# Attention and two gated layers on one core: how v of a pair of heads is brought into SBUF

## Chip, cores and metric

The kernel runs on one core of one Trainium2 chip. The metric is the device time of one execution in microseconds (us), as the median of several runs. A profile is one more execution, recorded instruction by instruction. Its span runs from the first instruction to the last, and its device time is a little longer than the span.

## What is computed

Three layers follow each other, on a batch of 4 sequences of 576 positions:

```python
# attention: 8 heads of 64, window of 128 positions, slope per head
scores = scale * np.matmul(q, k.transpose(0, 1, 3, 2))
scores = np.where((rel >= 0) & (rel < 128), scores + bias[None], -1e9)
attn = softmax(scores)                    # along the keys
x = np.matmul(attn, v)                    # heads side by side: 4 x 576 x 512
# first gated layer, 512 -> 1024 -> 512
h = np.maximum(x @ w_in, 0.0)
x = h * sigmoid(conv3(h)) @ w_out         # conv3: 3 taps along the sequence
# second gated layer, 512 -> 512 -> 512
out = sigmoid(conv5(x)) * (x @ w_val) @ w_out2   # conv5: 5 taps, causal
```

All inputs and the output are float32.

## The kernel before

**Units.** The work is cut into eight units (b, u): each of the 4 sequences in two parts, the second a little shorter or longer than the first. A unit goes through attention, `hidden` (w_in, ReLU, 3 taps, gate), `mixed` (w_out, 5 taps), `valued` (w_val and gate) and `output` (w_out2). While PE runs the dense layers of one unit, the attention of the next unit is interleaved with it.

**Dense layers.** `dense` and `prod` (L825 to L844) make each float32 product out of three matmuls of a high part and a low part: L830, L831 and L832 (`pm<-x,win`, `pm<-g,wout` and so on). ACT, DVE and POOL then work on the result: ACT scales (L415, L416, L432), DVE adds taps (L422) and, for a few taps, POOL adds them (L433, from a product that ACT made). At the end POOL makes the low part of the next operand (L437, `g<-t,g`), which PE needs for its L831 matmuls.

**Attention.** The first sequence uses `attention` (one pair of heads at a time, v loaded by L593). The other three use `duo`: two pairs of heads, r and its neighbour, at once. A unit has two duos, so there are 12 of them. One duo:

- q and k of two pairs are loaded (L697), into a ring of four buffers `qk`, two in the tile `qkt` and two in the tile `pp`.
- v of the two pairs is loaded into the tile `vr`, by two transfers (L715). Each chunk is 64 positions of the sequence. The 64 partitions 0 to 63 hold the first pair of heads, 64 to 127 the second. The two transfers take the even and the odd chunks. A duo of the first part has 5 chunks (3 and 2, that is 192 KB and 128 KB), one of the second part 6 (192 KB twice).
- POOL scales `vr` in place (L718, `vr<-vr,vup`), casts it to 16 bits (L408 through `cast`, `v<-vr`) and takes the remainder (L721, `v<-vr,v`). Both halves lie in `v16`. There is one `vr` and one `v16`: the next duo's transfers wait until L721 has read `vr`, and the next cast until the PV product has read `v16`.
- PE makes scores (L754), DVE and ACT the softmax (L564, L569, POOL L573 and DVE L575), ACT and DVE the two 16 bit halves of the probabilities (L781, L783), and two DMA transposes for each section (L788, `pp<-pp`) turn them. PE then makes the PV product (L811), which ACT and DVE move into x (L556, L558).

In DRAM v has the layout `vN[b, position in a block of 128, pair of heads, block, two heads x 64]`, so that each row is contiguous over the blocks of a pair.

**What sets the order.** Nothing is scheduled by the hardware across engines: every engine takes its instructions in the order of the program, and waits where a semaphore says so. A planner (`Program`) makes this order. Every operation is added with the engines that may run it, an assumed duration, and what it reads and writes. `forward` simulates a list schedule with assumed latencies, `backward` sets priorities from it, and `order` does so 1 + TRIES times, from the ninth time on with random changes of the priorities. The 12 shortest are replayed with random delays, and the best of these is the program. All transfers are issued by SP: `sync` (L401) takes an assumed transfer time, which it multiplies by 1.33, and an assumed issue time of SP, 475 ns unless given. In the assumption a transfer occupies one common DMA resource for its transfer time, whatever its shape.

POOL, too, is one queue: where L718 waits for v, the L433, L437, L408 and L573 behind it wait as well.

Of the kernel before, what the change touches and what calls it, by code (L numbers as in the profile page):

```python
# [26 lines left out]
TURN = 1  # L27
FILL = 80000.0
RW = 2 * WC
TRIES = 100  # L30
NATIVE = ()
LATE = (11,)

# [11 lines left out]
class Program:  # L45
# [165 lines left out]
    def order(self):  # L211
# [4 lines left out]
        rng, found = random.Random(1), []  # L216
        for i in range(1 + TRIES):
            if i:
# [64 lines left out]
def pool_t(n, two=False, ap=0):  # L283
    return 2.06 * n + 185 if two else 0.83 * n + 83 * ap + 160
# [15 lines left out]
def attention_moe_moe_kernel(  # L300
# [14 lines left out]
    nc = tc.nc  # L315
# [10 lines left out]
    def st(name, shape, dt):  # L326
        return sb.tile(shape, dt, name=name)
# [41 lines left out]
    vr = st("vr", [128, 6, 128], F32)  # L369
# [31 lines left out]
    def sync(fn, prio, reads=(), writes=(), xfer=0.0, issue=475.0):  # L401
        return pg.add("SP", issue, fn, prio, reads, writes, 0.0, xfer * 1.33)
# [275 lines left out]
    def users(keys):  # L678
        return {o for k in keys for o in [pg.writer.get(k)] + pg.readers.get(k, []) if o is not None}

    def duo(b, u, r, prio, step):
# [7 lines left out]
        early = prio - 3.149 * step * 2  # L689
        q_t, k_t, qk = [], [], []  # L690
        for y in range(2):
            t, key = ring_qd.next()
            old = users(QALIAS[ring_qd.at]) if ring_qd.i <= len(ring_qd.t) else set()
            first_, then = qk0[b, 2 * r + y], qk1[b, 2 * r + y]
            parts = [(0, 768, first_, 0), (768, 832, then, 768), (832, 960, then, 0)] if u == 0 else [(0, 960, then, 128)]
            for x, (a, e, src, f) in enumerate(parts):
                sync(lambda t=t, a=a, e=e, src=src, f=f: nc.sync.dma_start(out=t[:, a:e], in_=src[:, f:f + e - a]),  # L697
                     early, (), ((key, x),) if u == 0 else tuple((key, z) for z in range(3)), (e - a) * 1.43, 600.0).preds.update(old)
            qk += [(key, z) for z in range(3)]
            q_t.append([t[:, 128 * i:128 * i + 128] for i in range(4)] + ([t[:, 832:960]] if u == 0 else []))  # L700
            k_t.append(t[:, 512:832] if u == 0 else t[:, 576:960])
# [6 lines left out]

        n = 128 * nch
        vin, va, vb = vr[:, 0:nch], v16[:, 0, 0:nch], v16[:, 1, 0:nch]  # L710
        vk = (("vf0", 0), ("vf0", 1))
        old_v = users(("vf0",)) if nth == 0 else set()
        for x in range(2):
            c, at_, m = k0 + x, x * odd, (odd, nch - odd)[x]
            sync(lambda c=c, at_=at_, m=m: nc.sync.dma_start(  # L715
                out=vr[:, at_:at_ + m], in_=vN[b, 64 * (c % 2):64 * (c % 2) + 64, 2 * r:2 * r + 2, c // 2:c // 2 + m, :].rearrange(
                    "k y t c -> y k (t c)")), early + 6000.0, (), (("vf0", x),), 182.0 * m, 600.0).preds.update(old_v)
        pg.add("POOL", pool_t(n, False, 1), lambda: nc.gpsimd.tensor_scalar(vin, vin, s_up, 0.0, op0=ALU.mult, op1=ALU.add),  # L718
               prio, ((VS[b], 1, 0), (VS[b], 1, 1)), vk)
        cast(vin, va, n, prio, vk, (("v16", 0),) + (("vf1",) if nth == 0 else ()), ("POOL",))  # L720
# [7 lines left out]
        old = users(PALIAS) if nth == 0 else set()  # L728
# [3 lines left out]
        for gi, g in enumerate(secs):  # L732
# [4 lines left out]
            for y in range(2):  # L737
                o, sk = held[y]
                c = 0
# [24 lines left out]
            a, e = items[0][2], items[-1][2] + 1  # L764
            turned_over(stt[:, 2, a:e], stt[:, 1, a:e], norm, pr, tuple((stk, 1, x[2]) for x in items), ((stk, 2, gi),))
            for y, i, n, s, nkey, _, sk, on in items:
# [4 lines left out]
                if nth in LATE and y:  # L771
                    t, tk = ring_t.next()
                    t = t[:, 0:nkey]
                    tc3 = t.rearrange("p (t c) -> p t c", c=64)
                    pg.add("ACT", act_t(nkey, True, 1), lambda s=s, t=t, ri=ri: nc.scalar.activation(
                        out=t, in_=s, func=AF.Copy, scale=ri), pr, (on, (stk, 2, gi)), (tk,), bank=sk)
                    cast(tc3, hi, nkey, pr, (tk,), (("P", 0, i, y),))
                    pg.add("POOL", pool_t(nkey, True), lambda tc3=tc3, hi=hi, lo=lo: nc.gpsimd.tensor_tensor(
                        out=lo, in0=tc3, in1=hi, op=ALU.subtract), pr, (tk, ("P", 0, i, y)), (("P", 1, i, y),))
                    continue  # L780
                pg.add("ACT", act_t(nkey, True, 1), lambda sc=sc, hi=hi, ri=ri: nc.scalar.activation(  # L781
                    out=hi, in_=sc, func=AF.Copy, scale=ri), pr, (on, (stk, 2, gi)), (("P", 0, i, y),), bank=sk).preds.update(old)
                pg.add("DVE", dve_t(nkey, 1), lambda sc=sc, hi=hi, lo=lo, ri=ri: nc.vector.scalar_tensor_tensor(  # L783
                    out=lo, in0=sc, scalar=ri, in1=hi, op0=ALU.mult, op1=ALU.subtract),
                    pr, (on, (stk, 2, gi), ("P", 0, i, y)), (("P", 1, i, y),), bank=sk).preds.update(old)
            ca, ce = max(0, 3 * g[0] - base), 3 * g[-1] + 3 - base
            for q in range(2):
                sync(lambda q=q, ca=ca, ce=ce: nc.sync.dma_start_transpose(  # L788
                    out=ptd[:, q, ca:ce, :], in_=pd[:, q, ca:ce, :].rearrange("p a c -> p (a c)")),
# [182 lines left out]
    def attentions(b, u, base, T):  # L972
        if b < TURN:
            for p in range(NP):
                attention(b, u, p, base + T * (p / NP * 0.72 + 0.081), T * 0.72 / NP / (len(BLK[b, u]) + 1))
            return
        for r in range(NP // 2):
            duo(b, u, r, base + T * (r / 2 * 0.72 + 0.081), T * 0.72 / 2 / (3 + u))
# [14 lines left out]
    t, todo = T0, UNITS  # L993
    for i, (b, u) in enumerate(todo):
        base = t
        for f in steps:
            t = f(b, u, t, rate)
# [86 lines left out]
```

## Time and profile before

| what | value |
|---|---|
| median of 3 runs | 467.54 us (lowest 467.28) |
| profiled execution | 470.1 us |
| its span | 468.3 us |
| mean granted clock of TensorE in it | 0.949 |
| PE busy | 415.5 us (89%) |
| DVE, ACT busy | 298.4 us, 298.5 us (64% each) |
| POOL busy | 231.3 us (49%) |

The engines are PE (TensorE matmuls), PEld (its weight loads), DVE (VectorE), ACT (ScalarE), POOL (GpSimd) and SP (SyncE, which issues all transfers here). A granted clock of 1.00 is TensorE's higher level, 2.4 GHz, and 0.50 the lower, 1.2 GHz; a number between is a mean over a stretch that has both. The DMA share is the mean busy share of the core's 16 DMA engines; over short stretches with transposes it can come out above 1. An arrow in square brackets names how long an engine sat idle before an instruction and what ended that.

### The profile page before, as it was taken

The numbers are of one execution on the slowest core, as the hardware profiler recorded it, in microseconds if no ns is written. First come the engines' busy times: TensorE is split into PE (matmuls) and PEld (weight loads), VectorE is DVE, ScalarE is ACT, GpSimd is POOL, SyncE is SP. The second block draws the span as 40 slices with busy tenths as digits, with TensorE's granted clock in tenths as the row PEclk, the third lists the DMA queues.
The fourth block names the chain that finished last, engine by engine and source line by source line (L and its number), as shares of the span: only waits on it lengthen the run. The fifth ranks groups of instructions, "written<-read, shape, count | busy, mean of one in ns | idle before, by whom it ended". The sixth has DMA issues, their size and how long they took to land.

```text
span 468.3 us, 10804 instructions
## 1 busy us (share of the span) xinstructions
PE 415.5 (89%) x3925; PEld 390.4 (83%) x3925; DVE 298.4 (64%) x930; ACT 298.5 (64%) x906; POOL 231.3 (49%) x360
## 2 busy tenths in 40 slices
PE   7899998999599769699795779999969799999997
PEld 6778888899489769699694679999958799999896
DVE  3689988598565577565744527795754648662651
ACT  5799997487456556466735337876755448753743
POOL 3589997156463065143372316533643617651632
PEclk9999999999979979799977979999999899999999
DMA  7878777675933939344793761617178181031001
GB/s 239 306 244 274 245 257 229 186 199 120 179 67 71 125 62 131 39 99 117 59 118 45 45 161 28 154 28 181 35 143 54 34 110 30 2 70 57 1 0 47
DMA packets 64197, 53.77 MB, mean 115 GB/s; under 512 B 43792, under 2 KB 56464, under 8 KB 64144
## 3 DMA queue, kind: packets, MB, share of 16 engines
q1 hardware_dynamic: 64144, 53.08, 51.7%
q8 instruction: 31, 0.51, 0.5%
q14 instruction: 22, 0.18, 0.1%
HBM read 38.51 MB, written 4.72 MB: 92 GB/s over the span
## 4 chain that ended last, share of the span: by engine, by line
PE 36%; DMA 14%; POOL 4%; ACT 2%; DVE 2%; issue 2%; SPq 0%; POOLq 0%; ACTq 0%; DVEq 0%
PE pm L830 11%; PE pm L831 11%; PE pm L832 11%; DMA vr<-in_vN 8%; DMA pp<-pp 6%; POOL v L721 2%; PE psx L811 2%; PE pss L754 1%; POOL v L408 1%; POOL g L437 1%; DVE t L422 1%; ACT t L415 1%; DVE pss L564 1%; ACT pp L781 1%; POOL vr L718 1%
## 5 line engine op out<-in xcount | busy, mean ns | idle before, releaser
L830 PE MATMUL pm<-x,win 128*128 128x264 f32 (+3 forms) x256 | 80.8, 316 | 7.8 <-DVE t L422 7.6
L831 PE MATMUL pm<-g,wout 128*128 128x262 f32 (+3 forms) x256 | 78.7, 307 | 7.9 <-POOL g L437 7.9
L830 PE MATMUL pm<-g,wout 128*128 128x262 f32 (+3 forms) x256 | 80.2, 313 | 0.1
L422 DVE SCALAR_TENSOR_TENSOR t<-pm,cc,t 128x318 f32<-128x318 f32 (+7 forms) x112 | 56.0, 514 | 34.9 <-ACT t L415 20.8
L832 PE MATMUL pm<-g,wout 128*128 128x262 f32 (+3 forms) x256 | 77.8, 304 | 0.0
L831 PE MATMUL pm<-x,win 128*128 128x264 f32 (+3 forms) x256 | 77.3, 302 | 0.0
L832 PE MATMUL pm<-x,win 128*128 128x264 f32 (+3 forms) x256 | 77.2, 302 | 0.0
L569 ACT ACTIVATE pss<-pss,st 128x192 f32<-128x192 f32 (+2 forms) x108 | 40.4, 374 | 30.6 <-DVE st L564 29.5
L830 PEld LDWEIGHTS pm<-x,win 128*128 128x128 f32 x256 | 49.5, 193 | 10.8 <-DVE t L422 8.6
L422 DVE SCALAR_TENSOR_TENSOR gts<-pm,cc,gts 128x258 f32<-128x258 f32 (+7 forms) x92 | 44.8, 509 | 20.4 <-POOL gts L433 18.0
L831 PEld LDWEIGHTS pm<-g,wout 128*128 128x128 f32 x256 | 50.7, 198 | 8.4 <-POOL g L437 8.4
L437 POOL TENSOR_TENSOR g<-t,g 128x318 fp32r<-128x318 f32 (+3 forms) x64 | 51.5, 812 | 4.8 <-ACT g L406 2.8
L830 PEld LDWEIGHTS pm<-g,wout 128*128 128x128 f32 x256 | 50.1, 196 | 3.5 <-issue 1.7
L832 PEld LDWEIGHTS pm<-g,wout 128*128 128x128 f32 x256 | 50.7, 198 | 0.0
L831 PEld LDWEIGHTS pm<-x,win 128*128 128x128 f32 x256 | 49.7, 194 | 0.0
L832 PEld LDWEIGHTS pm<-x,win 128*128 128x128 f32 x256 | 49.4, 193 | 0.0
L433 POOL TENSOR_TENSOR gts<-gts,t 128x317 f32<-128x317 f32 (+3 forms) x36 | 29.0, 814 | 39.5 <-ACT t L432 23.9
L830 PE MATMUL pm<-g,wval 128*128 128x318 f32 (+3 forms) x128 | 41.6, 325 | 7.1 <-ACT pss L569 5.5
L781 ACT ACTIVATE pp<-pss,st 128x192 f16<-128x192 f32 (+2 forms) x104 | 35.4, 406 | 16.6 <-issue 14.2
L831 PE MATMUL pm<-g,wo 128*128 128x318 f32 (+3 forms) x128 | 38.9, 304 | 5.9 <-POOL g L437 5.7
L783 DVE SCALAR_TENSOR_TENSOR pp<-pss,st,pp 128x192 f16<-128x192 f32 (+2 forms) x104 | 36.8, 387 | 10.9 <-ACT pp L781 10.6
L874 ACT ACTIVATE t<-t 128x318 f32<-128x318 f32 (+3 forms) x64 | 28.2, 447 | 20.9 <-DVE t L422 20.8
(108 smaller groups left out, 1112.2 us busy)
## 6 DMA issues: line engine op xcount, KB each, us to landing
raw<-in_w_out SPq DMA_DIRECT2D x12, 512.0 KB
raw<-in_w_in SPq DMA_DIRECT2D x8, 512.0 KB, 3.2
qkt<-in_qk SPq DMA_DIRECT2D x10, 384.0 KB, 4.7
vr<-in_vN SPq DMA_DIRECT2D x18, 192.0 KB
qkt<-in_qk SPq DMA_DIRECT2D x6, 480.0 KB
pp<-in_qk SPq DMA_DIRECT2D x6, 480.0 KB, 5.4
raw<-in_vN SPq DMA_DIRECT2D x6, 384.0 KB, 6.2
pp<-in_qk SPq DMA_DIRECT2D x6, 384.0 KB
```

Source lines behind the costliest of these rows:

```text
L422: pg.add("DVE", dve_t(n, 0 if isinstance(scalar, float) else 1), lambda: nc.vector.scalar_tensor_tensor(out=out, in0=in0, scalar=scalar, i ...
L433: pg.add("POOL", pool_t(n, True), lambda: nc.gpsimd.tensor_tensor(out=out, in0=out, in1=t, op=ALU.add), prio, (tk,), (key,))
L437: "POOL": (pool_t(n, True), lambda: nc.gpsimd.tensor_tensor(out=lo, in0=src, in1=hi.bitcast(F32), op=ALU.subtract))}
L569: pg.add("ACT", act_t(nkey, True, 2), lambda: nc.scalar.activation(out=to, in_=s, func=AF.Exp, scale=-1.0, bias=best, accum_out=total), pr ...
L721: pg.add("POOL", pool_t(n, True), lambda: nc.gpsimd.tensor_tensor(out=vb, in0=vin, in1=va, op=ALU.subtract), prio, vk + (("v16", 0),), ((" ...
L781: pg.add("ACT", act_t(nkey, True, 1), lambda sc=sc, hi=hi, ri=ri: nc.scalar.activation(out=hi, in_=sc, func=AF.Copy, scale=ri), pr, (on, ( ...
L783: pg.add("DVE", dve_t(nkey, 1), lambda sc=sc, hi=hi, lo=lo, ri=ri: nc.vector.scalar_tensor_tensor(out=lo, in0=sc, scalar=ri, in1=hi, op0=A ...
L811: m.append(nc.tensor.matmul(out=o, lhsT=v16[64 * y:64 * y + 64, pv, c, 64 * h:64 * h + 64], rhs=rhs, start=n == 0, stop=n == len(mms) - 1, ...
L830: return [nc.tensor.matmul(out=o, lhsT=wh, rhs=hi, start=first, stop=False), nc.tensor.matmul(out=o, lhsT=wh, rhs=lo, start=False, stop=Fa ...
L831: nc.tensor.matmul(out=o, lhsT=wh, rhs=lo, start=False, stop=False),
L832: nc.tensor.matmul(out=o, lhsT=wl, rhs=hi, start=False, stop=last)]
L874: pg.add("ACT", act_t(Ng), lambda c=c: nc.scalar.activation(out=c, in_=c, func=AF.Tanh, scale=0.5), pr, (), (ak,))
```

## The change

`duo` loads v with four transfers instead of two: for the even and the odd chunks, and for each of the two pairs of heads, one transfer of 64 partitions. The source of one such transfer has the 64 positions as its outermost dimension; before, the source was rearranged to "pair, position, chunk x columns", with the pair, of size 2, outermost. Each of the four is a key of its own for the planner, with half the assumed transfer time and the same assumed issue time of 600 ns. The bytes and where they land are the same. Beside this, the assumed issue time of a q or k transfer of `duo` goes from 600 to 475 ns, and the planner tries 300 orders instead of 100.

```diff
--- before.py
+++ after.py
@@ -27,7 +27,7 @@
 TURN = 1
 FILL = 80000.0
 RW = 2 * WC
-TRIES = 100
+TRIES = 300
 NATIVE = ()
 LATE = (11,)
 
@@ -695,7 +695,7 @@
             parts = [(0, 768, first_, 0), (768, 832, then, 768), (832, 960, then, 0)] if u == 0 else [(0, 960, then, 128)]
             for x, (a, e, src, f) in enumerate(parts):
                 sync(lambda t=t, a=a, e=e, src=src, f=f: nc.sync.dma_start(out=t[:, a:e], in_=src[:, f:f + e - a]),
-                     early, (), ((key, x),) if u == 0 else tuple((key, z) for z in range(3)), (e - a) * 1.43, 600.0).preds.update(old)
+                     early, (), ((key, x),) if u == 0 else tuple((key, z) for z in range(3)), (e - a) * 1.43).preds.update(old)
             qk += [(key, z) for z in range(3)]
             q_t.append([t[:, 128 * i:128 * i + 128] for i in range(4)] + ([t[:, 832:960]] if u == 0 else []))
             k_t.append(t[:, 512:832] if u == 0 else t[:, 576:960])
@@ -708,13 +708,15 @@
 
         n = 128 * nch
         vin, va, vb = vr[:, 0:nch], v16[:, 0, 0:nch], v16[:, 1, 0:nch]
-        vk = (("vf0", 0), ("vf0", 1))
+        vk = tuple(("vf0", x, y) for x in range(2) for y in range(2))
         old_v = users(("vf0",)) if nth == 0 else set()
         for x in range(2):
             c, at_, m = k0 + x, x * odd, (odd, nch - odd)[x]
-            sync(lambda c=c, at_=at_, m=m: nc.sync.dma_start(
-                out=vr[:, at_:at_ + m], in_=vN[b, 64 * (c % 2):64 * (c % 2) + 64, 2 * r:2 * r + 2, c // 2:c // 2 + m, :].rearrange(
-                    "k y t c -> y k (t c)")), early + 6000.0, (), (("vf0", x),), 182.0 * m, 600.0).preds.update(old_v)
+            for y in range(2):
+                sync(lambda c=c, at_=at_, m=m, y=y: nc.sync.dma_start(
+                    out=vr[64 * y:64 * y + 64, at_:at_ + m],
+                    in_=vN[b, 64 * (c % 2):64 * (c % 2) + 64, 2 * r + y, c // 2:c // 2 + m, :]),
+                    early + 6000.0, (), (("vf0", x, y),), 91.0 * m, 600.0).preds.update(old_v)
         pg.add("POOL", pool_t(n, False, 1), lambda: nc.gpsimd.tensor_scalar(vin, vin, s_up, 0.0, op0=ALU.mult, op1=ALU.add),
                prio, ((VS[b], 1, 0), (VS[b], 1, 1)), vk)
         cast(vin, va, n, prio, vk, (("v16", 0),) + (("vf1",) if nth == 0 else ()), ("POOL",))
```

## Rows read from the trace of the kernel before

**Rows 1.** The page, busy time: us, share of the span, instructions.
```profile
PE 415.5 (89%) x3925; PEld 390.4 (83%) x3925; DVE 298.4 (64%) x930; ACT 298.5 (64%) x906; POOL 231.3 (49%) x360
```
**Rows 2.** Windows, 110 to 390 us: length, busy us (instructions), clock, DMA share, GB/s.
```profile
core 0: us, PE busy (x) PEld busy (x) DVE busy (x) ACT busy (x) POOL busy (x), PEclk, DMA share, GB/s
110.00:390.00 280.00, 241.21 (x2463) 227.94 (x2456) 168.74 (x539) 166.31 (x528) 119.13 (x172) 0.91 0.55 91
```
**Rows 3.** Waits of PE from 110 to 390 us: total, times, longest.
```profile
PE pm L831 <- POOL g L437: 13.7, 3, 5.7
PE psx L811 <- DMA pp<-pp: 12.8, 5, 5.2
PE pm L830 <- DVE t L422: 6.2, 1, 6.2
PE pm L830 <- ACT pss L569: 5.5, 1, 5.5
```
**Rows 4.** Waits of POOL over the whole span.
```profile
POOL vr L718 <- DMA vr<-in_vN: 60.5, 9, 12.2
...
POOL v L408 <- PE pss L811: 8.2, 4, 2.7
```
**Rows 5.** Timelines of POOL, DVE and PE around one stall: start, us, what.
```profile
123.07 0.80 POOL L718 TENSOR_SCALAR vr<-vr,vup 128x640 f32<-128x640 f32 x1 [8.34 <-DMA vr<-in_vN]
...
127.72 0.55 DVE L422 SCALAR_TENSOR_TENSOR gts<-pm,cc,gts 128x322 f32<-128x322 f32 x1 [5.52 <-POOL gts L433]
...
129.16 0.61 PE L830 MATMUL pm<-g,wval 128*128 128x322 f32 x1 [5.55 <-ACT pss L569]
```
**Rows 6.** The chain in order of time, 215 to 272 us, and one SP issue.
```profile
224.27 8.88 DMA vr<-in_vN
...
240.50 1.16 SPq L715 DMA_DIRECT2D vr<-in_vN x2
...
243.14 10.43 DMA pp<-pp
...
259.57 10.28 DMA vr<-in_vN
```
**Rows 7.** Windows of 1 us (columns as in rows 2), and SP's issues at 300.71.
```profile
248.00:249.00 1.00, 0.46 (x7) 0.18 (x6) 0.28 (x2) 1.00 (x3) 0.00 (x0) 1.00 0.14 49
...
300.71 1.62 SPq L697 DMA_DIRECT2D pp<-in_qk x3
...
301.00:302.00 1.00, 1.00 (x9) 1.00 (x8) 0.35 (x2) 0.62 (x3) 0.08 (x1) 1.00 1.02 397
```
**Rows 8.** Windows that begin where PE starts again after idle time.
```profile
129.16:137.00 7.84, 7.47 (x34) 7.09 (x35) 5.93 (x14) 4.61 (x12) 5.08 (x8) 0.67 0.37 64
...
271.70:280.00 8.30, 8.30 (x42) 8.30 (x43) 1.57 (x5) 3.36 (x11) 0.19 (x1) 0.64 0.62 153
349.83:356.00 6.17, 6.17 (x39) 6.17 (x40) 1.58 (x5) 2.00 (x6) 3.65 (x5) 0.76 0.37 107
366.71:372.00 5.29, 5.29 (x45) 5.17 (x45) 4.42 (x15) 3.73 (x14) 3.99 (x4) 0.70 0.01 4
438.07:446.00 7.93, 7.93 (x65) 7.93 (x66) 4.66 (x11) 5.57 (x14) 5.80 (x9) 1.00 0.01 2
```
**Rows 9.** Issues: L715's duration (ns) on SP; landing of L941, L504 (88 to 96 us), L788.
```profile
L715 SPq DMA_DIRECT2D vr<-in_vN x24: 506/552/692, 68.9 to 370.8; - x24
...
DMA to landing us min/median/max: 1.7/1.9/2.1
...
raw<-in_vN SPq DMA_DIRECT2D x3, 384.0 KB, 3.9
...
DMA to landing us min/median/max: 2.8/3.6/6.7
```
**Rows 10.** Window from 280 to 300 us (columns as in rows 2).
```profile
280.00:300.00 20.00, 20.00 (x221) 19.11 (x220) 16.94 (x48) 15.56 (x47) 13.15 (x21) 1.00 0.24 47
```

## Prediction

> **What bounds the kernel now.** I read the page first, then the windows, the waits of PE and of POOL, the timelines around one stall, the chain in order of time, and last the DMA rates. The page says that PE is busy 415.5 of 468.3 us, so PE is idle for 52.8 us in all, and no other engine comes near it [rows 1]. The windows show where: from 110 to 390 us, which is where the batches that use `duo` run, PE is busy 241.21 of 280 us at a mean granted clock of 0.91 [rows 2]. PE's waits in that stretch have four large entries: POOL g L437 with 13.7 us, DMA pp<-pp with 12.8, DVE t L422 with 6.2 and ACT pss L569 with 5.5, 38.2 us together [rows 3]. They are eight stalls: three behind L437, three behind transposes (in five pieces, one of them 0.2 us), one and one.
>
> They look like four causes and are one. POOL's longest wait by far is vr L718 for the v transfer, 60.5 us in nine times [rows 4]. POOL works in order, so behind the waiting L718 stand the additions (L433) and subtractions (L437) that feed DVE, ACT and PE. The timelines show it for the stall that PE's waits put down to ACT: L718 starts at 123.07 after 8.34 us of waiting; a DVE tap, idle for 5.52 us, starts only at 127.72 because its POOL addition came late; PE starts at 129.16 after 5.55 us [rows 5]. The 6.2 us stall behind DVE t L422 has the same form, after L718's longest wait, 12.2 us [rows 4]. The chain shows the other two forms: the v transfer takes 8.88 us from 224.27 and 10.28 us from 259.57, each followed by POOL L718, L437 and PE; and a transpose chain of 10.43 us begins at 243.14, after v was issued at 240.50 [rows 6].
>
> Why the transfers are slow is in the DMA columns. While v alone is in flight (248 to 249 us) the DMA share is 0.14 and 49 GB/s move; while transfers of q and k run (301 to 302 us; three of them are issued from 300.71 on) the share is 1.02 and 397 GB/s move [rows 7]. Two of sixteen engines is 0.125, and the source's outermost dimension is the pair of heads. The transposes use all engines, so their pieces on those two stand behind v.
>
> A stall has a second price. After PE starts again, the granted clock is at the lower level, 1.2 GHz, for some microseconds. In eight windows, each from a restart to where the clock is whole again, the mean clock is 0.64 to 0.76; busy time times (1 - clock) is 2.47, 2.22, 2.74, 2.68, 1.85, 2.99, 1.48 and 1.59, in all 18.0 us; the first, the largest, the smallest and the last of the eight stand in [rows 8]. The ninth window, after an idle of 1.10 us, keeps 1.00 [rows 8]: short gaps cost no clock.
>
> **The change part by part.** The edit replaces two transfers per duo with four of 64 partitions, 96 KB or 64 KB each, whose outermost dimension on both sides is 64 partitions. There are 12 duos, so 24 more issues on SP. One costs 0.552 us [rows 9], so 13.2 us of SP in all, 1.1 us per duo. SP computes nothing; what stands behind the four issues is the next transpose or transfer, which leaves 1.1 us later.
>
> How long four such transfers take the trace does not show, so I bound it. Counted from the end of the first issue, as the chain counts, the fourth is issued 3 x 0.55 = 1.7 us later. It then lands after 1.9 us if it is like the output stores (median of L941), or after 3.9 us if it is like the 384 KB that L504 loads from the same tensor with 128 partitions [rows 9]. That is 3.6 to 5.6 us; I take the middle, 4.6, since L504 carries all of the bytes in one transfer and each store only a part of a tile. Today the four v pieces on the chain last 8.88 and 10.28 [rows 6] and two more of the same kind, so some 9.2; the gain is 4.6 us per stall, between 3.6 and 5.6.
>
> What of the eight stalls is left? Of the five on POOL, 5.55 leaves 1.0, 6.2 leaves 1.6, and the three of 13.7 us in all (longest 5.7 [rows 3]) leave 1.1 from the longest and nothing from the others, which are under 4.6. The three on transposes end when a transpose lands as it does alone, 3.6 us in the median [rows 9], instead of the 10.43 of [rows 6]; even 1.1 us later on SP that is 5.7 us less, more than the 5.2 us of the longest such stall; the shortest of these chains leaves some 0.4. So 4.1 us of 38.2 stay and 34.1 go. The gaps left are 1.6 us or less, nearer to the 1.10 that cost no clock than to those that did, so I count all 18.0 us of clock as gained. With the gain at its low end of 3.6, the five keep about 7 us instead of 3.7; at its high end, 1.
>
> Would another engine stop PE as soon as v does not? The stretch from 280 to 300 us, where v arrived before POOL needed it, runs PE 20.00 of 20 us at clock 1.00, with DVE busy 16.94, ACT 15.56 and POOL 13.15 [rows 10]. So the other engines can feed a PE that never stops, with 15% of DVE to spare.
>
> The remaining edits act on the planner alone. It assumes 475 ns instead of 600 for a q or k issue, keeps 600 for each of four v issues, with half the transfer time in each, and tries 300 orders instead of 100. No instruction becomes shorter by this, but the order of the whole program is drawn anew. No row gives its price. All idle time of PE that is not v's is 52.8 - 38.2 = 14.6 us; I bound the new order by doubling that (+14.6) and by halving it (-7.3), and take nothing.
>
> Sum, against the profiled execution's 470.1 us: 470.1 - 34.1 - 18.0 = 418.0. The median of the runs is 467.54, 0.9946 of it, so 415.7; I say 416 us.
>
> **The rivals.** First, the cast takes the wait's place (chance 0.11). There is only one v16, and POOL's cast into it (L408) has to wait until the PV product before has read it: 8.2 us today in four waits, longest 2.7 [rows 4]. If POOL comes to it sooner, it waits there, with the same work queued behind. At 2.7 us in each of eight stalls, 21.6 us of idle stay; gaps of that size lie between the 1.10 without and the stalls with a clock loss, so half of the 18.0 stays too: 470.1 - 16.6 - 9.0 = 444.5, or 442 on the median. For it speaks that POOL is in order; against it, that the planner knows this dependency and places the cast after the product.
>
> Second, the four transfers go one after another, each with its own fixed time. At 1.9 us each [rows 9] the last lands after 7.6 instead of 9.2: 1.6 x 8 = 12.8 us of idle go, and a third of the clock loss: 470.1 - 12.8 - 6.0 = 451.3, or 449. Against it stand q and k: with several short transfers from the same queue in flight, 397 GB/s move, so they follow each other without a pause [rows 7]; chance 0.06. The Trainium skill, page "DMA: Bandwidth & Descriptors", section "Rules for kernel authors", advises against two transfers to disjoint partition halves, since they serialize on the same engines, and wants one transfer of 128 partitions; taken strictly, it would make this 449 the time.
>
> Third, the same mechanism on the other side: one after another, and each as slow as L504's 3.9 us [rows 9]. Then the last lands after 15.6 us, 6.4 us later than today, in eight places: 470.1 + 51 = 521, or 518 us. The point that decides is 9.2 / 4 = 2.3 us per transfer; above it the change loses. Against it stands again the rate of [rows 7]. Chance 0.04.
>
> Fourth, the change does not do what it says: the transfers stay on two engines, because something else confines them. The bytes are the same, so the time stays at 468, with 1.1 us more of SP per duo that v's own landing covers. Chance 0.05; against it, the transfers of 128 partitions from the same tensor land in 3.9 us.
>
> **How the numbers follow.** The forecast has 0.74. Its own range is 408 (new order 7.3 better) to 434 (14.6 worse and the transfers at their slow end). The range asked for goes from 407 to 442, to take in the first rival, and leaves out the other three and the far ends, about 0.2. A measurement of this kernel can tell some 2% from no change, 9.4 us, so faster means under 458: forecast and the first two cases, 0.91. Same is the fourth, 0.05; slower the third, 0.04.
>
> **What would show it.** In the profile after: POOL's wait of L718 for v well under 20 us instead of 60.5; no stretch of several microseconds with a DMA share of 0.13; the v DMA gone from the chain; PE's waits for transposes under 3 us; a mean clock of 0.98 or more instead of 0.949 over the span; PE's idle time under 25 us. The forecast is wrong if L718 still waits 5 us per duo, if L408's wait for the PV product grows past 20 us, or if the clock still dips after 110 us with PE waiting for DVE or ACT for a reason that does not lead back to v.

## The result and the profile after

The changed kernel takes 409.39 us (median of 4 runs, 408.45 to 409.93) against 467.49 for the kernel before: a ratio of 0.8756 with a 95% interval of 0.8735 to 0.8777. The forecast was 416 us, the range 407 to 442. Ratios in this document leave out runs that are over 1.5% above the fastest of the same kernel, here one of 764.05 us of the kernel before; medians keep them.

The page of the changed kernel, with busy times, the chain by engine and the new transfers of 96 KB (count, size, median us from issue to landing), answers to [rows 1]. Line numbers behind the edit are 2 higher than before: L832 to L834 are the three products, L720 is POOL's scaling of v, L716 v's transfers, L790 the transposes, L813 the PV product.

```profile
span 406.7 us, 10818 instructions
...
PE 396.0 (97%) x3921; PEld 373.4 (92%) x3921; DVE 301.0 (74%) x940; ACT 296.9 (73%) x904; POOL 229.0 (56%) x352
...
PE 80%; ACT 8%; DVE 7%; DMA 1%; issue 1%; SPq 1%; POOL 1%; DVEq 0%; POOLq 0%; ACTq 0%
...
vr<-in_vN SPq DMA_DIRECT2D x36, 96.0 KB, 2.7
```

The span fell by 61.6 us. Of this, 42.1 us are idle time of PE (468.3 - 415.5 = 52.8 before, 406.7 - 396.0 = 10.7 now), and 19.5 us are PE's own busy time, 415.5 to 396.0, with as many matmuls but for four: the mean granted clock of the span is 1.000 now, against 0.949. The other engines do the work they did, and their busy times hardly differ. The window over the duos answers to [rows 2]; it is 230 us long now, PE is idle for 0.46 us of it, and the clock is whole:

```profile
core 0: us, PE busy (x) PEld busy (x) DVE busy (x) ACT busy (x) POOL busy (x), PEclk, DMA share, GB/s
110.00:340.00 230.00, 229.54 (x2458) 217.94 (x2457) 176.20 (x562) 170.28 (x538) 124.99 (x181) 1.00 0.48 107
```

The waits of PE over the whole span (total, times, longest) answer to [rows 3]. None of the four large entries of before is left; the longest total is a wait of the first 60 us that was there before, and the last line shown is what remains of the wait for DVE's taps.

```profile
PE psx L1013 <- DVE x L552: 1.9, 4, 0.6
PE psx L1013 <- DVE one L948: 1.1, 1, 1.1
PE pss L641 <- POOL pp L630: 1.0, 3, 0.4
PE pm L832 <- DVE t L422: 0.7, 2, 0.4
```

The waits of POOL answer to [rows 4]: L720's wait for v went from 60.5 us to 6.7, and the cast's wait for the PV product, the first rival, fell too, from 8.2 to 2.7. The wait for the scale of v (`vup`) grew from 1.7 us to 7.9; it ends at 189.90 us, inside the stretch in which PE is idle for 0.46 us in all, so it costs PE next to nothing.

```profile
POOL vr L720 <- DVE vup L527: 7.9, 1, 7.9
POOL vr L720 <- DMA vr<-in_vN: 6.7, 3, 4.2
...
POOL v L408 <- PE pss L813: 2.7, 3, 1.5
```

The windows of half a microsecond while the four transfers issued at 239.54 are in flight answer to [rows 7]. The share is 0.38 to 0.51 and 121 to 155 GB/s move, some three times the 49 of before, but a third of the 388 that q and k reach (205 to 206 us). A share of 0.51 is more than eight of sixteen engines; that all sixteen take part, no window shows.

```profile
241.00:241.50 0.50, 0.50 (x5) 0.50 (x4) 0.50 (x2) 0.50 (x3) 0.06 (x2) 1.00 0.42 145
241.50:242.00 0.50, 0.50 (x6) 0.50 (x5) 0.50 (x2) 0.50 (x2) 0.42 (x2) 1.00 0.38 121
242.00:242.50 0.50, 0.50 (x5) 0.50 (x5) 0.50 (x2) 0.50 (x3) 0.50 (x1) 1.00 0.51 155
```

SP's issues of v (duration in ns: least, median, most) and their landing over both sizes answer to [rows 9]. Four issues take 2.4 us of SP.

```profile
L716 SPq DMA_DIRECT2D vr<-in_vN x48: 465/587/597, 68.3 to 312.6; - x48
...
DMA to landing us min/median/max: 2.2/2.5/5.3
```

The same of the transposes, first of the kernel before, then of the changed one. A transpose lands after 3.3 us in the median and 5.2 at most, instead of 3.6 and 6.7 [rows 9]. Its issue changed too: before, SP took up to 4.7 us for one, now 1.8 at most. So behind a slow v the transposes were held up on SP as well, and what SP issues next with them.

```profile
L788 SPq DMA_TRANSPOSE pp<-pp x48: 1210/1249/4721, 95.1 to 414.5; - x48
...
L790 SPq DMA_TRANSPOSE pp<-pp x48: 1209/1232/1794, 85.4 to 352.8; - x48
...
DMA to landing us min/median/max: 2.7/3.3/5.2
```

### The profile page after: what moved, and what is told of

It is laid out like the page before. It is cut to its first block, busy times and chain, and to the rows that moved or that the text cites. A ratio compares the mean times of both kernels' runs of the same rounds, so it can differ in the third digit from the quotient of the medians.

```text
span 406.7 us, 10818 instructions
## 1 busy us (share of the span) xinstructions
PE 396.0 (97%) x3921; PEld 373.4 (92%) x3921; DVE 301.0 (74%) x940; ACT 296.9 (73%) x904; POOL 229.0 (56%) x352
## 4 chain that ended last, share of the span: by engine, by line
PE 80%; ACT 8%; DVE 7%; DMA 1%; issue 1%; SPq 1%; POOL 1%; DVEq 0%; POOLq 0%; ACTq 0%
PE pm L832 24%; PE pm L833 22%; PE pm L834 22%; PE pss L756 4%; PE psx L813 2%; DVE pss L564 2%; PE psx L1013 2%; PE pss L615 1%; ACT pp L569 1%; DVE t L422 1%; DMA vr<-in_vN 1%; ACT pm L459 1%; PE pss L641 1%; PE psx L668 1%; DVE gts L422 1%
## 5 line engine op out<-in xcount | busy, mean ns | idle before, releaser
L832 PE MATMUL pm<-x,win 128*128 128x264 f32 (+3 forms) x256 | 78.4, 306 | 0.7 <-DVE t L422 0.7
L832 PE MATMUL pm<-g,wout 128*128 128x262 f32 (+3 forms) x256 | 78.3, 306 | 0.5 <-ACT pp L632 0.5
L833 PE MATMUL pm<-g,wout 128*128 128x262 f32 (+3 forms) x256 | 76.2, 298 | 0.0
L834 PE MATMUL pm<-x,win 128*128 128x264 f32 (+3 forms) x256 | 75.9, 297 | 0.0
L833 PE MATMUL pm<-x,win 128*128 128x264 f32 (+3 forms) x256 | 75.9, 297 | 0.0
L834 PE MATMUL pm<-g,wout 128*128 128x262 f32 (+3 forms) x256 | 75.8, 296 | 0.0
L422 DVE SCALAR_TENSOR_TENSOR t<-pm,cc,t 128x318 f32<-128x318 f32 (+7 forms) x112 | 56.9, 515 | 22.2 <-ACT t L415 19.4
L437 POOL TENSOR_TENSOR g<-t,g 128x318 fp32r<-128x318 f32 (+3 forms) x64 | 51.7, 813 | 24.5 <-ACT g L406 22.9
L832 PEld LDWEIGHTS pm<-g,wout 128*128 128x128 f32 x256 | 48.1, 188 | 3.7 <-issue 2.2
L832 PEld LDWEIGHTS pm<-x,win 128*128 128x128 f32 x256 | 48.1, 188 | 2.7 <-DVE t L422 1.4
L833 PEld LDWEIGHTS pm<-g,wout 128*128 128x128 f32 x256 | 48.6, 190 | 0.0
L834 PEld LDWEIGHTS pm<-g,wout 128*128 128x128 f32 x256 | 48.5, 189 | 0.0
L833 PEld LDWEIGHTS pm<-x,win 128*128 128x128 f32 x256 | 48.3, 189 | 0.0
L834 PEld LDWEIGHTS pm<-x,win 128*128 128x128 f32 x256 | 48.2, 188 | 0.0
L832 PE MATMUL pm<-g,wval 128*128 128x318 f32 (+3 forms) x128 | 39.4, 308 | 0.7 <-DVE gts L422 0.3
L564 DVE CUSTOM_DVE_ANT_0 pss<-pss,bm 128x192 f32<-128x192 f32 (+2 forms) x90 | 30.9, 347 | 12.1 <-PE pss L615 5.5
L832 PE MATMUL pm<-g,wo 128*128 128x318 f32 (+3 forms) x128 | 38.6, 302 | 0.0
```

Of the source, the lines that this page charges most:

```text
L422: pg.add("DVE", dve_t(n, 0 if isinstance(scalar, float) else 1), lambda: nc.vector.scalar_tensor_tensor(out=out, in0=in0, scalar=scalar, i ...
L437: "POOL": (pool_t(n, True), lambda: nc.gpsimd.tensor_tensor(out=lo, in0=src, in1=hi.bitcast(F32), op=ALU.subtract))}
L564: pg.add("DVE", 75 + 1.05 * nkey, lambda: nc.vector.tensor_tensor_reduce(out=s, in0=s, in1=tab[:, 192 - nkey:192], op0=ALU.add, op1=ALU.mi ...
L832: return [nc.tensor.matmul(out=o, lhsT=wh, rhs=hi, start=first, stop=False), nc.tensor.matmul(out=o, lhsT=wh, rhs=lo, start=False, stop=Fa ...
L833: nc.tensor.matmul(out=o, lhsT=wh, rhs=lo, start=False, stop=False),
L834: nc.tensor.matmul(out=o, lhsT=wl, rhs=hi, start=False, stop=last)]
```

## The experiments

Three theories stood against each other. Theory 1: the number of DMA engines that a transfer gets decides, and all eight stalls come from it. Theory 2: the newly drawn order of the program brings the gain. Theory 3: smaller transfers with releases of their own bring it.

**The new transfers in the old order.** `same_order` is the kernel before with one planner operation issuing two of the new transfers, so that its order is the old one.

```diff
-            sync(lambda c=c, at_=at_, m=m: nc.sync.dma_start(
-                out=vr[:, at_:at_ + m], in_=vN[b, 64 * (c % 2):64 * (c % 2) + 64, 2 * r:2 * r + 2, c // 2:c // 2 + m, :].rearrange(
-                    "k y t c -> y k (t c)")), early + 6000.0, (), (("vf0", x),), 182.0 * m, 600.0).preds.update(old_v)
+            sync(lambda c=c, at_=at_, m=m: [nc.sync.dma_start(
+                out=vr[64 * y:64 * y + 64, at_:at_ + m],
+                in_=vN[b, 64 * (c % 2):64 * (c % 2) + 64, 2 * r + y, c // 2:c // 2 + m, :]) for y in range(2)],
+                early + 6000.0, (), (("vf0", x),), 182.0 * m, 600.0).preds.update(old_v)
```

> Theory 1 (number of DMA engines per transfer): the order of the kernel before with four transfers of 64 partitions loses the v stalls; median 410 to 420 us, POOL's wait of L718 for v under 20 us, clock 0.98 or more. Theory 2 (the newly drawn order brings the gain): within 2% of 467 us, L718 still waiting some 60 us.

It took 415.07 us, a ratio of 0.8909 (0.8875 to 0.8942). Its page:

```profile
PE 399.8 (97%) x3925; PEld 376.5 (91%) x3925; DVE 297.3 (72%) x930; ACT 298.1 (72%) x906; POOL 231.5 (56%) x360
```

POOL's wait for v:

```profile
POOL vr L719 <- DMA vr<-in_vN: 13.7, 5, 6.3
```

PE's waits for DVE's taps:

```profile
PE pm L831 <- DVE gts L422: 2.0, 3, 1.2
PE pm L831 <- DVE t L422: 1.4, 2, 1.1
```

As theory 1 has it: without one change to the order, 60.5 us of waiting become 13.7, and 465.54 us, the kernel before in the same comparison, become 415.07. PE no longer waits for a transpose at all, and for POOL's L437 0.7 us. The waits for DVE's taps that are left, 3.4 us together and none over 1.2, are the size of what the prediction let stay.

**The planner's edits alone.** `plan_only` keeps the two transfers of before.

```diff
-TRIES = 100
+TRIES = 300
...
-                     early, (), ((key, x),) if u == 0 else tuple((key, z) for z in range(3)), (e - a) * 1.43, 600.0).preds.update(old)
+                     early, (), ((key, x),) if u == 0 else tuple((key, z) for z in range(3)), (e - a) * 1.43).preds.update(old)
```

> v stays in two transfers with the pair outermost; only the 300 tries and the assumed 475 ns for q and k. Theory 1: 455 to 480 us, DMA share 0.13 while v is in flight, L718 waiting 45 us or more. Theory 2: 409 to 420 us.

459.87 us, 0.9873 (0.9831 to 0.9915): 1.3% less, which is clear of the spread of the runs but under the 2% that the prediction counts as a change. POOL waits for v as long as ever:

```profile
POOL vr L718 <- DMA vr<-in_vN: 60.6, 9, 12.2
```

And on its page PE is busy as long as before, so the clock is no better:

```profile
PE 415.5 (90%) x3915; PEld 389.5 (85%) x3915; DVE 300.2 (65%) x939; ACT 297.9 (65%) x910; POOL 226.3 (49%) x347
```

So theory 2 is wrong as the main cause, but the order seems to have a part. The two parts multiply to the whole: 0.8909 x 0.9873 = 0.8796, and the changed order with the new transfers measured 0.8784 in the same comparison (next run).

**Two runs that changed nothing.** `outer2` and `outer8` meant to confine the new transfers by writing the 64 positions as 2 x 32 or 8 x 8.

```diff
-                    in_=vN[b, 64 * (c % 2):64 * (c % 2) + 64, 2 * r + y, c // 2:c // 2 + m, :]),
+                    in_=vN[b, 64 * (c % 2):64 * (c % 2) + 64, 2 * r + y, c // 2:c // 2 + m, :].rearrange(
+                        "(a k) t c -> a k (t c)", a=2)),
```

> The changed kernel, its order kept, four transfers of 64 partitions, but each source written as 2 x 32 positions, so that the outermost dimension is 2 again. Theory 1: the DMA share falls to 0.13 again, v lands after 8 to 10 us, 455 to 485 us. Theory 3 (the smaller transfers or their four separate releases bring the gain): 409 to 412 us.

> As outer2 but 8 x 8 positions outermost. Theory 1: eight engines, DMA share near 0.5, the four land 1 to 2 us later than in the changed kernel; 409 to 416 us. Theory 3: 409 us, no difference in the landing.

They took 408.84 and 409.41 us (0.8784, 0.875 to 0.8817, and 0.8793, 0.876 to 0.8825), and a 96 KB transfer landed after 2.7 and 2.9 us as in the changed kernel. So `outer2` missed what theory 1 expected of it, 455 to 485 us. It does not speak for theory 3 either: with v in flight its DMA share is 0.42 to 0.49 (241.5 to 243 us), so nothing was confined to two engines. The two new dimensions have one common stride, so they can be carried as the one dimension of 64 that they were; that they were is inferred from this share. For `outer8` both theories allowed 409 us, so it decides nothing. I take the two as more measurements of the changed kernel. To confine a transfer, its outermost dimension must be one that can't be merged.

**Four transfers on two engines.** `four_pairs` has the changed kernel's order and four transfers, but each takes half of the chunks of both pairs, with the pair outermost, so they carry 64 or 128 KB. The pair and the position have different strides, so here nothing should merge.

```diff
-                sync(lambda c=c, at_=at_, m=m, y=y: nc.sync.dma_start(
-                    out=vr[64 * y:64 * y + 64, at_:at_ + m],
-                    in_=vN[b, 64 * (c % 2):64 * (c % 2) + 64, 2 * r + y, c // 2:c // 2 + m, :]),
...
+                e0, e1 = (0, m - m // 2) if y == 0 else (m - m // 2, m)
+                sync(lambda c=c, at_=at_, e0=e0, e1=e1: nc.sync.dma_start(
+                    out=vr[:, at_ + e0:at_ + e1], in_=vN[b, 64 * (c % 2):64 * (c % 2) + 64, 2 * r:2 * r + 2, c // 2 + e0:c // 2 + e1, :].rearrange(
...
```

> The changed kernel's order, and four transfers of 64 or 128 KB, but each with the pair of heads outermost (they split the chunks instead of the pair). Theory 1 (number of engines): DMA share 0.13 while v is in flight, v landing after 6 us or more, stalls behind L718 and the transposes back, 440 to 475 us. Theory 3 (smaller transfers with four releases bring the gain): 409 to 413 us.

464.56 us, 0.9957 (0.9919 to 0.9995): nearly all of the gain is lost. A window with v in flight:

```profile
258.00:259.00 1.00, 1.00 (x10) 1.00 (x9) 0.00 (x0) 0.00 (x0) 0.00 (x0) 1.00 0.14 46
```

The wait of POOL for v:

```profile
POOL vr L720 <- DMA vr<-in_vN: 55.9, 9, 10.8
```

The waits of PE:

```profile
PE pm L832 <- ACT t L415: 10.0, 3, 4.3
PE pm L833 <- POOL g L437: 8.6, 2, 4.6
PE psx L813 <- DMA pp<-pp: 8.1, 3, 4.2
PE pm L832 <- ACT t L432: 5.8, 1, 5.8
```

The share is 0.14 again, and with it come all forms of the stall: behind POOL, behind the transposes, and under ACT's name. DVE, ACT and POOL are busy 0.00 us in that window, and PE uses up its last work: it stops at 259.39 us and starts again at 263.69, while L720, waiting for v, starts at 261.16. Theory 3 is out: the number of transfers and the releases are those of the changed kernel.

**A scale of engines.** Each v transfer is cut in two along the partitions, at 62, 57, 49 or 32. The two pieces are issued one behind the other, eight per duo; only the cut differs.

```diff
-                sync(lambda c=c, at_=at_, m=m, y=y: nc.sync.dma_start(
-                    out=vr[64 * y:64 * y + 64, at_:at_ + m],
-                    in_=vN[b, 64 * (c % 2):64 * (c % 2) + 64, 2 * r + y, c // 2:c // 2 + m, :]),
+                sync(lambda c=c, at_=at_, m=m, y=y: [nc.sync.dma_start(
+                    out=vr[64 * y + p0:64 * y + p1, at_:at_ + m],
+                    in_=vN[b, 64 * (c % 2) + p0:64 * (c % 2) + p1, 2 * r + y, c // 2:c // 2 + m, :]) for p0, p1 in ((0, 62), (62, 64))],
```

> The changed kernel with each v transfer cut into one of 62 partitions and one of 2. Theory 1 in the form that the number of engines must divide the outermost size (62 is 2 x 31): two engines carry almost all bytes, share 0.13, 440 to 475 us. Theory 1 in the form that only an outermost size under 16 confines a transfer: 409 to 415 us, the same as with a cut at 32. The Trainium skill, page DMA: Bandwidth & Descriptors, section on why a DMA increments its semaphore by 16, states the first form.

> The changed kernel with each v transfer cut at 57 partitions (57 is 3 x 19). If the number of engines divides the outermost size: three engines, share 0.19, about 73 GB/s, and a time between split62 (453 us) and split32 (410 us): 420 to 447 us. If split62 was slow for another reason (small odd pieces of few partitions): 450 us as well.

> The same with a cut at 49 (49 is 7 x 7, 15 is left). If the number of engines divides the outermost size: seven engines, share 0.44, some 170 GB/s, so that v lands some 1 to 2 us later than in split32: 410 to 418 us. If odd pieces are the reason: 450 us.

> The changed kernel with each v transfer cut into two of 32 partitions: eight issues per duo, 4.7 us of SP instead of 2.3. If the issues on SP are covered, as the forecast has it: 409 to 413 us. If transfers to disjoint partitions go one after another with a fixed time each (second rival): v lands some 4 us later, 415 to 435 us.

| cut | largest divisor up to 16 of the big piece | DMA share and GB/s with v in flight | L720's wait put down to v, and to other transfers, us | median, us | ratio |
|---|---|---|---|---|---|
| 62 + 2 | 2 | 0.13, 49 | 33.6, 16.7 | 453.09 | 0.9699 (0.9651 to 0.9747) |
| 57 + 7 | 3 | 0.20, 74 | 21.6, 7.7 | 423.48 | 0.9084 (0.9029 to 0.914) |
| 49 + 15 | 7 | 0.26 to 0.52, 61 to 153 | 6.5, 4.2 | 409.98 | 0.8803 (0.876 to 0.8846) |
| 32 + 32 | 16 | 0.26 to 0.44, 66 to 120 | 8.5, 4.2 | 410.13 | 0.8787 (0.8742 to 0.8833) |

In the last two the share changes from one half microsecond to the next (242 to 245 us and 244 to 247.5 us, v alone in flight), so the number of engines can't be read from it. The windows for the first two, v in flight. First the cut at 62:

```profile
255.00:255.50 0.50, 0.50 (x5) 0.50 (x5) 0.00 (x0) 0.00 (x0) 0.00 (x0) 1.00 0.13 49
```

Then the cut at 57:

```profile
218.00:218.50 0.50, 0.50 (x6) 0.50 (x5) 0.50 (x3) 0.00 (x0) 0.47 (x1) 1.00 0.20 74
```

Two sixteenths are 0.125 and three 0.1875; 49 and 74 GB/s are 24.5 and 24.7 per engine. So for these two the number of engines is the largest divisor up to 16 of the outermost size, not "all sixteen if there are enough rows", and the time follows it. The Trainium skill, page "DMA: Bandwidth & Descriptors", section "Why a DMA increments its semaphore by 16 and not by 1", states this rule (the largest number up to 16 that divides the outermost sizes of both sides); these two runs agree. Small odd pieces are no reason, since the cut at 49 costs nothing. The cut at 49 came out just below its 410 to 418 us: from seven engines on there is no gain. An estimate says why. At 24.5 each, seven engines would carry 172 GB/s, but SP takes 2.82 us for the eight issues of 384 KB at that cut (241.22 us), which is 139 GB/s at most, and 0.59 us for 96 KB (98,304 bytes) in the changed kernel, which is 167; there v moves at 121 to 155. That SP's issue rate is the limit is worked out from these numbers, not tried.

The cut at 32 also prices SP's issues: twice as many of them, which take 3.59 us per duo instead of 2.40 (not the 4.7 that was expected), cost nothing that can be measured against 408.84 to 409.41. The Trainium skill, page "DMA: Bandwidth & Descriptors", section "Rules for kernel authors", says that transfers to disjoint partition halves serialize and are not worth it. This further cut agrees in so far as it brought nothing; the cut of the change itself is worth 50 us (465.54 to 415.07 in `same_order`), because the one transfer it replaces ran on two engines.

Left open: `four_pairs` and `split62` both run on two engines, and the second is 11 us faster. L720's waits for transfers are nearly as long in it, 50.3 us (33.6 for v, 10.6 put down to q and k, 6.1 to a load of v for its scale) against 55.9, and I have not tried what makes the difference.

**Idle transfers behind v.** `shadow` and `shadow2` start from `same_order`, where v is fast. In 9 of the 12 duos they add two transfers of the old form, which bring the same bytes once more into a tile that nobody reads any more.

```diff
+            def loads(x=x, c=c, at_=at_, m=m, done=done):
...
+                done.append(x)
+                if nth >= 3 and len(done) == 2:
+                    sh = ring_raw.t[0][:, 0:768].bitcast(F32).rearrange("p (a c) -> p a c", c=128)
+                    for z in range(2):
+                        c_, a_, m_ = k0 + z, z * odd, (odd, nch - odd)[z]
+                        nc.sync.dma_start(out=sh[:, a_:a_ + m_], in_=vN[b, 64 * (c_ % 2):64 * (c_ % 2) + 64, 2 * r:2 * r + 2,
+                                                                        c_ // 2:c_ // 2 + m_, :].rearrange("k y t c -> y k (t c)"))
...
```

> As same_order (four transfers in the order of the kernel before), and in 9 of the 12 duos, behind v, two more transfers of the old form (pair outermost) bring the same bytes to a tile that nobody reads. If transposes stand behind the pieces on the two engines, PE's wait for pp<-pp comes back with 5 to 13 us and the time is 420 to 435 us, though L718 waits no longer than in same_order. If only POOL's wait for v mattered: 413 to 418 us.

`shadow` took 452.82 us (0.9701, 0.9645 to 0.9757), above both expectations. PE waited 23.0 us for the transposes, but POOL's wait for v rose to 41.4 us, against what was expected. SP's timeline shows why: in three duos the idle pair went out between the two halves of v, since the planner had put the odd chunks first there.

```profile
221.12 1.16 SPq L717 DMA_DIRECT2D vr<-in_vN  x2
222.33 1.14 SPq L723 DMA_DIRECT2D raw<-in_vN  x2
223.52 2.90 SPq L717 DMA_DIRECT2D vr<-in_vN  x2
```

So it mixes the two effects and decides nothing about the share of each; `shadow2` issues the idle pair behind all of v (the diff above is its own).

> As shadow, but the two idle transfers of the old form are always issued behind all four of v, never between them. If transposes stand behind the pieces on the two engines: PE's wait for pp<-pp 8 to 25 us against none in same_order, L718 waiting for v not much over the 13.7 us of same_order, 425 to 450 us. If only POOL's wait for v mattered: 413 to 418 us.

447.8 us, 0.9529 (0.9426 to 0.9632); its runs spread from 441.18 to 449.79. The ratio counts those of 441.18 and 446.95, and the profile is of one at 448.64. Its longest wait of PE:

```profile
PE psx L821 <- DMA pp<-pp: 26.3, 5, 8.6
```

Its waits of POOL:

```profile
POOL v L408 <- PE pss L821: 22.9, 6, 8.2
POOL vr L728 <- DMA vr<-in_vN: 16.3, 5, 6.2
```

The issue and the landing of its transposes:

```profile
L798 SPq DMA_TRANSPOSE pp<-pp x48: 1209/1238/5868, 93.9 to 393.1; - x48
...
DMA to landing us min/median/max: 2.8/5.8/11.1
```

POOL waits for v hardly longer than in `same_order` (16.3 against 13.7), PE waits for no POOL subtraction, and yet some 30 us are lost (0.9529 - 0.8909 of 467 is 29; the medians differ by 33): transposes land after 5.8 us in the median instead of 2.8 and up to 11.1 instead of 5.1, and SP took up to 5.9 us to issue one instead of 1.9. One of the waits shows it: PE stands idle for a transpose from 229.27 to 237.51 us, and from 231 to 236 us the DMA share is 0.13 and 49 GB/s move. Two engines' worth of transfer is at work, and bandwidth is not short. So a transfer that nobody waits for delays what is issued behind it. That it does so because it fills two engines that a transpose needs fits these numbers, but idle transfers on sixteen engines, which would separate this from the extra bytes, were not tried; the two extra issues themselves, 1.15 us of SP, are no more than what `split32` added at no cost. Behind the late PV product the first rival shows up too: the cast waits 22.9 us for it.

**The size of the search.** `tries100` is the changed kernel with 100 orders.

```diff
-TRIES = 300
+TRIES = 100
```

> The changed kernel with 100 orders tried instead of 300. If the 6 us between same_order (415 us) and the changed kernel come from the larger search: 412 to 416 us. If they come from the planner's other numbers (four v transfers, 475 ns for q and k): 408 to 411 us.

411.03 us (410.61 to 412.8; ratio 0.8828, 0.8787 to 0.8868), between the two expectations. Of the 6 us between `same_order` and the changed kernel, some 4 come from the planner's other numbers, the four transfers with their issue times and the cheaper q and k, which were not tried apart. Some 2 are left for the larger search (411.03 against 408.84 to 409.41), no more than the spread of the runs.

## Why the prediction was right

**Diagnosis.** Four names, one cause: right. `same_order` removes all four large entries of PE's waits by v's transfers alone, and `four_pairs` brings stalls of the same kinds back, in part under other names. One thing the prediction did not see: it has the transposes wait on the engines behind v, but SP's issue of them was held up as well, up to 4.7 us for one.

**Two engines.** Right, and the scale of cuts shows it: with 2 and 3 engines the time is 453 and 423 us, and with what should be 7 and 16 it is 410.

**The time of the four transfers.** Estimated at 4.6 us from the end of the first issue, from bounds of 3.6 and 5.6. By the medians of the changed kernel, three more issues of 0.59 us and a landing after 2.7 us make 4.5. Not every one was so quick: on the chain one landed 4.90 us after the third issue, 6.2 us after the first, with transfers of q and k and a transpose issued just ahead:

```profile
297.52 0.48 SPq L716
...
299.33 4.90 DMA vr<-in_vN
```

It cost POOL 1.92 us and PE nothing.

**The stalls.** 34.1 of 38.2 us were to go. In `same_order`, with the old order, 2.9 us of idle are left from 110 to 350 us, near the 4.1 that were to stay; in the changed kernel 0.46.

**The clock.** 18.0 us were to come back; PE's busy time fell by 19.5, and by 15.7 in `same_order` (415.5 to 399.8), whose order is the old one. The count of what the lower clock had cost, busy time times what the clock lacked, was good to some 2 us. The stalls that are left are short and, as row 438.07 of [rows 8] had it, cost no clock: in `same_order` it is 1.00 from 110 to 350 us, with 2.9 us of idle in it.

**SP.** 24 more issues were put at 1.1 us per duo, covered. Four issues took 2.40 us of SP where two had taken 1.14, so 1.3 us more per duo. Twice as many issues, in `split32`, cost nothing measurable.

**The new order.** This is the term that was mis-sized: it was taken as nothing, with -7.3 and +14.6 as bounds, and it is worth 5.7 to 6.2 us in both comparisons (465.54 to 459.87 with the old transfers, 415.07 to 409.41 and 408.84 with the new). Without it the forecast of 416 stands beside 415.07. That this is so close is in part luck: by the profiles PE's idle time in `same_order` fell by 39.1 us instead of 34.1, and its busy time by 15.7 instead of 18.0, and the two misses partly cancel. For the new order the prediction had no row, and took nothing; its bounds held.

**The rivals.** The cast did not take the wait's place in the changed kernel, where the products came on time; it did in `shadow2`, where they came late. The four transfers did not go one after another: with 2.7 us each that would be 10.8 us, against 4.5. The signs that were named held, except one: v is still on the chain, with 1%.

## What to carry to other kernels

A wait that a profile puts down to ACT, DVE, POOL and a transpose in turn can be one slow transfer: look at the DMA share while it is alone in flight, since a small constant fraction (here 0.13 with 49 GB/s) says that it runs on a few engines. Make the outermost dimension of a transfer one whose size has a large divisor up to 16, even if that takes more transfers. And mind transfers with slack too: here one on two engines held up the transposes issued behind it.

## What the runs showed of the hardware

- For two odd sizes the number of DMA engines was the largest divisor up to 16 of the number of partitions: 62 partitions ran at a share of 0.13 (two engines), 57 at 0.20 (three), some 24.5 GB/s per engine.
- Transfers that no instruction waits for cost some 30 us here (`shadow2` against `same_order`), through the transposes queued behind them: these landed after 5.8 us in the median instead of 2.8, and SP took up to 5.9 us to issue one instead of 1.9.
- A cut that should give 7 engines was as good as one that should give 16 (409.98 and 410.13 us), with 2.82 and 3.59 us of SP for eight issues of 384 KB in all.
- An issue on SP took 0.55 us for a v transfer of two engines and up to 192 KB, 0.59 us for one of 64 partitions and 0.42 us for one of 32 partitions (medians).
